# Weight sums in 28 steps on VectorE over two chunks, the split two periods ahead of its inverse, and gelu written into the products' tile

## The chip, the cores and the metric

The kernel runs on one core of a Trainium2 chip. The metric is the device time of one execution in microseconds, lower is better. A core has five engines, each with its own queue of instructions, kept in order: TensorE (PE, matmuls; its weight loads run beside it), VectorE (DVE), ScalarE (ACT), GpSimd (POOL) and SyncE (SP), which here only issues DMAs. Engines wait for each other by semaphores. PE writes into PSUM, whose eight banks are reused; everything else lies in SBUF.

## The reference

One block over 8192 tokens of width 448: adaptive layer norm, a spectral mixer (2D FFT, a two-layer block MLP in the frequency domain, inverse FFT), a residual, a second layer norm, and a gated feed-forward net of width 1792.

```python
sa, ca, ga, sb, cb, gb = (silu(c) @ w_mod) in six parts
h = layernorm(x) * (1 + ca) + sa
x = x + ga * irfft2(block_mlp(rfft2(h)))
h = layernorm(x) * (1 + cb) + sb
x = x + gb * ((gelu(h @ w_gate) * (h @ w_up)) @ w_down)
```

## The kernel before

The first part (forward transform, MLP in frequency, first half of the inverse) ends at about 385 us of the profile, and the change doesn't touch it. The second part runs over 32 chunks of 256 tokens (`CB` = 2 rows of 128 by `nch` = 32). For each chunk it does the second half of the inverse transform, the residual and the layer norm; it casts the result to a high and a low f16 part (`pack_hi`, `pack_lo`, tile `pk`), transposes it by DMA into `nt` (tiles of 128 columns at the places `UN`, `NU` of them), multiplies by the gate and up weights (high part `wh`, low part `wl`), and by the down weights. Products are made of f16 pairs: high by high, high by low, low by high.

The 1792 columns are seven pairs `t` of two blocks of 128. Two ways are used for gate and up:

- The first four chunks (`C0` = 4) are plain: `gate_up(i, k)` over 14 steps k, then `gate_up_out`: gelu on ScalarE (L1215, into a tile `gel`), the product gate by up on VectorE (L1224, into a tile `x` of eight blocks), and four sums of blocks on GpSimd (`out_sums`, L1232 to L1235). `quantize` makes the f16 pair of a finished `x`: the high part on ScalarE (L1240), the low part on VectorE (L1244).
- From the fifth chunk on, each 2 by 2 block product takes seven products in place of eight (Strassen's scheme). It needs sums of the input blocks (`combos`) and of the weight blocks (tiles `sh`). `period(n, hook)` is the unit of this part: pair n enters with `front1` and `front2`, pair n-1 passes `mid`, pair n-2 finishes with `back_e` and `back_d` (gelu, product, sums of each half), and pairs n-3 and n-4 are quantized. The PSUM banks go round in a ring with three E and three D slots: `front1` can take its E slot only when the product on VectorE of the period before has read it.

`down(i-1)` (seven products of the down weights, output stored at L1466) is written after step k = 2 of a plain chunk and after the period t = 2 of a later one.

The weight sums for the seven products are made once. `make_s` (four 128x128 adds on GpSimd, L1398 to L1401, then a high part on ScalarE, L1391, and a low part of 384 columns on VectorE, L1392) runs at the steps of chunk 2, and `make_s1` (one add, L1404, its result written over weights in `wh` and `wl` that plain chunks no longer need) at those of chunk 3 and in the first period. 42 loads of raw weights (L1388) go through SyncE into a tile `rc` of two buffers.

What else a chunk needs is placed by hand. `hooks` holds, by step k, what is done in plain chunks for later chunks; `hooks2` does so for the periods, where k = 2t + j, with j = 0 after `mid` and j = 1 at the end of the period. An entry's first number says how many chunks ahead it works. `split_g` and `split_v` cast the inverse's operand and take its low part on ScalarE (L123) and GpSimd (L125: `gl`, `vn`); `inverse` is L1036 to L1038. `transposes_dma` (L1146) puts the transposes of the next chunk into SyncE's queue; in later chunks 16 of 22 go at k = 4, and six behind the output store. SyncE works its queue in order, so each transfer waits for those issued ahead of it, and each of those for its buffer.

Of the kernel before, what the change touches and what calls it, by code (L numbers as in the profile page):

```python
# [39 lines left out]
NU = 24  # L40
UN = [0, 2, 16, 18, 20, 8, 10, 22]
# [18 lines left out]
def spectral_geglu(ctx, tc, x, wt_in, wgu, wd, cvec, wmod, cf1, cs2, cmi, cgm, out):  # L60
# [924 lines left out]
    with ExitStack() as cctx:  # L985
# [4 lines left out]
        cp.tile([128, H], F32, tag="gel", name="gel", bufs=2)  # L990
# [17 lines left out]
        def x8():  # L1008
            return cp.tile([128, 8, 128], F32, tag="x8", name="x8", bufs=3)
# [106 lines left out]
        def pack_lo(i):  # L1116
# [10 lines left out]
            if i > 0:  # L1127
                nt_tile(i)
# [7 lines left out]
        def transposes_dma(i, lo=0, hi=None):  # L1136
            todo = [(UN[t] + b, source(i, t, b)) for t in range(8) for b in range(2) if i < C0 or (t, b) not in ((0, 1), (5, 1))]
            if i >= C0:
                pk = nxt[i]["pk"]
                todo += [  # L1140
                    (8 * l + 4 + j, pk[:, l * NF + 2 * D + j * 128 : l * NF + 2 * D + (j + 1) * 128])
                    for l in range(2)
                    for j in range(4)
                ]
# [66 lines left out]
        gels = {}  # L1211

        def out_gelu(i, t, q, ps):
            gl = cp.tile([128, H], F32, tag="gel", name="gel", bufs=2)
            S.activation(gl, ps[:, :H], AF.Gelu_apprx_tanh, scale=dg)  # L1215
            gels[(i, t, q)] = gl

        def out_mult(i, t, q, ps):
            gl = gels.pop((i, t, q))
            if (i, t) not in acts:  # L1220
                acts[(i, t)] = x8()
            x = acts[(i, t)]
            dst = x[:, 1:3] if q else x[:, 0::7]
            V.tensor_tensor(  # L1224
                dst, ps[:, H : 2 * H].rearrange("p (b c) -> p b c", b=2), gl.rearrange("p (b c) -> p b c", b=2), ALU.mult
            )
# [47 lines left out]
        def prod(c, ps, b, w, u, start=False):  # L1274

            nt = nts[c[0]]
            for pr in range(2):
                o = ps[:, pr * H + b * 128 : pr * H + (b + 1) * 128]
                for n, (l, v) in enumerate(((0, u), (0, u + 8), (1, u))):
# [38 lines left out]
        def front1(a):  # L1318
# [4 lines left out]
            prod(a, e, 0, a_of(t, 1, 0), 4)  # L1323
# [5 lines left out]
        def front2(a):  # L1329
            prod(a, es[a], 1, s_of(a[1], 0), 5)  # L1330
            V.tensor_tensor(quarter(ds[a], 1), quarter(es[a], 1), c5s[a], ALU.add)  # L1331

        def mid(b):
            e = es[b]
            prod(b, e, 1, s_of(b[1], 2), 6)
# [3 lines left out]
        def back_e(c):  # L1339
            e = es[c]  # L1340
            prod(c, e, 0, a_of(c[1], 1, 1), 7)
# [16 lines left out]
        def period(n, hook):  # L1358
# [25 lines left out]
        def load_s(t, pr, lo):  # L1384
            raws_s[(t, pr)] = r = sp.tile([128, 512], F32, tag="rc", name="rc", bufs=2).rearrange("p (i k c) -> p i k c", i=2, k=2)
            for i in range(lo, 2):
                m = t + NP * i
                dma(r[:, i], wgu[m // 2, pr, :, 0:2, (m % 2) * 128 : (m % 2) * 128 + 128])  # L1388

        def w_split(hi, lo, src, pr):  # L1390
            S.activation(hi, src, AF.Copy, scale=sw[:, pr : pr + 1])  # L1391
            V.scalar_tensor_tensor(lo, src, sw[:, pr : pr + 1], hi, op0=ALU.mult, op1=ALU.subtract)  # L1392

        def make_s(t, pr):
            r = raws_s.pop((t, pr)).rearrange("p i k c -> p (i k) c")
            if pr == 0:
                shs[t] = sp.tile([128, 2, 2, 3, 128], F16, name=f"sh{t}")
            G.tensor_tensor(r[:, 3], r[:, 2], r[:, 3], ALU.add)  # L1398
            G.tensor_tensor(r[:, 2], r[:, 0], r[:, 2], ALU.subtract)
            G.tensor_tensor(r[:, 0], r[:, 3], r[:, 0], ALU.subtract)  # L1400
            G.tensor_tensor(r[:, 1], r[:, 1], r[:, 0], ALU.subtract)  # L1401
# [305 lines left out]
```

## Time and profile before

| | us |
|---|---|
| median of 3 runs | 2112.77 |
| lowest and highest run | 2112.22, 2117.72 |
| the profiled execution's own time | 2107.65 |
| span of the profile, first to last instruction | 2105.9 |
| mean granted TensorE clock, share of full | 0.957 |

In the profile's page an engine's row tells its busy time, its share of the span, and its instructions. A string of 40 digits cuts the span into equal slices, each digit the busy share in tenths. Rows of waits say which line of an engine waited, for which line of which engine, how long in total, how often, and the longest. Rows of a timeline give start, length, engine, line, operation, output from input, and in brackets the idle time ahead and what ended it.

### The profile page before, as it was taken

The numbers are of one execution on the slowest core, as the hardware profiler recorded it, in microseconds if no ns is written. First come the engines' busy times: TensorE is split into PE (matmuls) and PEld (weight loads), VectorE is DVE, ScalarE is ACT, GpSimd is POOL, SyncE is SP. The second block draws the span as 40 slices with busy tenths as digits, with TensorE's granted clock in tenths as the row PEclk, the third lists the DMA queues.
The fourth block names the chain that finished last, engine by engine and source line by source line (L and its number), as shares of the span: only waits on it lengthen the run. The fifth ranks groups of instructions, "written<-read, shape, count | busy, mean of one in ns | idle before, by whom it ended". The sixth has DMA issues, their size and how long they took to land.

```text
span 2105.9 us, 51710 instructions
## 1 busy us (share of the span) xinstructions
PE 1940.9 (92%) x21137; PEld 1706.1 (81%) x21137; DVE 1298.7 (62%) x2877; ACT 981.3 (47%) x1942; POOL 1252.8 (59%) x1591
## 2 busy tenths in 40 slices
PE   7899999896676999999999999999999999999998
PEld 3689999685465888888888888888888888888897
DVE  8687898772525555666655655665566556655544
ACT  6677887431323444444444444444444444444433
POOL 4466796353754566666665666666666666666544
PEclk9899999898888999999999999999999999999999
DMA  9988786411121111111111111111111111111100
GB/s 389 289 273 236 206 229 173 127 41 53 57 63 48 45 44 44 44 54 45 45 45 45 53 50 49 44 44 44 44 44 44 44 45 44 45 44 45 26 19 19
DMA packets 182739, 175.95 MB, mean 84 GB/s; under 512 B 112614, under 2 KB 155366, under 8 KB 182118
## 3 DMA queue, kind: packets, MB, share of 16 engines
q1 hardware_dynamic: 182502, 172.65, 27.8%
q8 instruction: 165, 2.70, 0.5%
q14 instruction: 72, 0.59, 0.1%
HBM read 103.79 MB, written 47.25 MB: 72 GB/s over the span
## 4 chain that ended last, share of the span: by engine, by line
PE 36%; POOL 28%; ACT 7%; DVE 5%; issue 3%; SPq 2%; DMA 1%; POOLq 0%; ACTq 0%
POOL x L1232 9%; PE pdn L1414 7%; PE pdn L1416 7%; PE pdn L1415 7%; PE ring L1280 6%; PE ring L1294 6%; ACT ac L1240 4%; POOL x L1233 4%; POOL pk L1126 3%; POOL x L1235 3%; DVE x L1224 3%; POOL vn L125 3%; ACT gel L1215 2%; SPq L1146 2%; POOL x L1234 2%
## 5 line engine op out<-in xcount | busy, mean ns | idle before, releaser
L1232 POOL TENSOR_TENSOR x<-x 128x128 f32<-128x128 f32 x223 | 275.9, 1237 | 328.5 <-DVE x L1224 320.2
L1414 PE MATMUL pdn<-wd,ac 128*128 128x224 f16 x1568 | 409.2, 261 | 23.9 <-ACT p L1445 18.1
L1416 PE MATMUL pdn<-wd,ac 128*128 128x224 f16 x1568 | 408.9, 261 | 6.5 <-DVE ac L1244 6.5
L1415 PE MATMUL pdn<-wd,ac 128*128 128x224 f16 x1568 | 409.1, 261 | 0.0
L1294 PE MATMUL ring<-nt,wh 128*128 128x256 f16 x2352 | 379.4, 280 | 0.0
L1224 DVE TENSOR_TENSOR x<-ring,gel 128x256 f32<-128x256 f32 x392 | 164.6, 420 | 308.7 <-ACT gel L1215 308.7
L1280 PE MATMUL ring<-nt,wh 128*128 128x128 f16 x3136 | 332.8, 222 | 11.2 <-DVE x L1224 11.2
L1244 DVE SCALAR_TENSOR_TENSOR ac<-x,sa_act,ac 128x896 f16<-128x896 f32 (+1 forms) x226 | 315.8, 1399 | 13.8 <-ACT ac L1240 13.8
L1280 PE MATMUL ring<-nt,sh 128*128 128x128 f16 x3528 | 298.6, 221 | 13.8 <-ACT rc L1327 13.6
L1240 ACT ACTIVATE ac<-x,sa_act 128x896 f16<-128x896 f32 (+1 forms) x226 | 233.9, 1036 | 141.4 <-POOL x L1235 141.2
L1280 PE MATMUL ring<-nt,wl 128*128 128x128 f16 x1568 | 298.7, 222 | 0.0
L1215 ACT ACTIVATE gel<-ring,dg 128x256 f32<-128x256 f32 x392 | 183.7, 469 | 197.9 <-PE ring L1309 163.3
L1280 PEld LDWEIGHTS <-wh 128*128 128x128 f16 x3136 | 251.9, 99 | 27.2 <-issue 23.7
L1280 PEld LDWEIGHTS <-sh 128*128 128x128 f16 x3528 | 217.3, 99 | 63.7 <-issue 63.7
L1294 PEld LDWEIGHTS <-wh 128*128 128x128 f16 x2352 | 220.3, 101 | 22.0
L1325 ACT COPY ring<-ring 128x256 f32<-128x256 f32 x196 | 70.0, 357 | 325.1 <-PE ring L1280 249.8
L1294 PE MATMUL ring<-nt,wl 128*128 128x256 f16 x784 | 219.3, 280 | 0.0
L1458 POOL TENSOR_TENSOR vo<-u,p 128x224 f32<-128x224 f32 x32 | 21.4, 668 | 298.0 <-DVE u L1457 298.0
L1415 PEld LDWEIGHTS <-ac 128*128 128x128 f16 x1568 | 154.5, 99 | 20.0 <-issue 18.3
L1331 DVE TENSOR_TENSOR ring<-ring,rc 128x256 f32<-128x256 f32 x196 | 84.4, 430 | 125.2 <-PE ring L1280 125.0
L1416 PEld LDWEIGHTS <-ac 128*128 128x128 f16 x1568 | 154.6, 99 | 8.6 <-DVE ac L1244 7.9
L1414 PEld LDWEIGHTS <-ac 128*128 128x128 f16 x1568 | 154.5, 99 | 7.6 <-ACT ac L1240 6.3
(313 smaller groups left out, 4385.4 us busy)
## 6 DMA issues: line engine op xcount, KB each, us to landing
raw<-in_gu SPq DMA_DIRECT2D x28, 512.0 KB, 5.3
vd<-us SPq DMA_DIRECT2D x64, 224.0 KB, 3.4
v<-vd SPq DMA_DIRECT2D x64, 224.0 KB, 2.8
x<-in_x SPq DMA_DIRECT2D x31, 448.0 KB, 4.5
out<-x SPq DMA_DIRECT2D x31, 448.0 KB, 2.6
nt<-pk SPq DMA_TRANSPOSE x656, 2.3
tr<-td SPq DMA_DIRECT2D x22, 448.0 KB, 7.0
tb<-in_x SPq DMA_DIRECT2D x8, 896.0 KB, 17.7
```

Source lines behind the costliest of these rows:

```text
L1215: S.activation(gl, ps[:, :H], AF.Gelu_apprx_tanh, scale=dg)
L1224: V.tensor_tensor(dst, ps[:, H : 2 * H].rearrange("p (b c) -> p b c", b=2), gl.rearrange("p (b c) -> p b c", b=2), ALU.mult)
L1232: e.tensor_tensor(s1, a21, a22, ALU.add)
L1233: e.tensor_tensor(s2, s1, a11, ALU.subtract)
L1240: S.activation(acq[(i, t)][:, 0, k], acts[(i, t)][:, k], AF.Copy, scale=sa_act[:, t : t + 1])
L1244: V.scalar_tensor_tensor(ac[:, 1, k], acts[(i, t)][:, k], sa_act[:, t : t + 1], ac[:, 0, k], op0=ALU.mult, op1=ALU.subtract)
L1280: T.matmul(o, w(l, pr), nt[:, v * 128 : (v + 1) * 128], start=start and pr == 0 and n == 0, stop=n == 2, skip_group_check=True,)
L1294: T.matmul(ps[:, pr * H : (pr + 1) * H], w[:, tw, f0 : f0 + 128], nt[:, UN[tn] * 128 : UN[tn] * 128 + H], start=False, stop=True, skip_gro ...
L1331: V.tensor_tensor(quarter(ds[a], 1), quarter(es[a], 1), c5s[a], ALU.add)
L1414: T.matmul(ps, ac[:, 0, ka], wds[t][:, 0, kb], start=t == 0, stop=False)
L1415: T.matmul(ps, ac[:, 0, ka], wds[t][:, 1, kb], start=False, stop=False)
L1416: T.matmul(ps, ac[:, 1, ka], wds[t][:, 0, kb], start=False, stop=t == NP - 1)
```

## The change

- **Weight sums.** All four sums of a pair get a place in `sh` (512 columns, the fourth is now `s_of(t, 3)`), so nothing in `wh` or `wl` is written over and `make_s1` is gone. The four adds run on VectorE. `sums_step` counts steps: an even one makes the high part of one sum and issues two loads for the next (28 in all), an odd one makes the low part. It is called at three places of `down(1)` and `down(2)`, at the steps 1 to 13 of chunk 2 and at the steps of chunk 3, 33 places for the 30 steps that are needed.
- **Gelu.** It is written straight into the products' tile `x`, and the product is taken in place. The tile `gel` is gone, and `x` has two buffers for three.
- **Plain chunks' transposes.** The next chunk's are issued four at a time at k = 0, 3, 5 and 7, the rest at k = 9, where all were issued at k = 0.
- **Later chunks.** The split is at k = 0 (period t = 0) for k = 2 (t = 1); the inverse stays at k = 4 (t = 2). `pack_hi` and `pack_lo` are at k = 10 and 11 (t = 5) for 12 and 13 (t = 6). `load_v` and `load_g` are written in another place, but stand at the same place in SyncE's queue.
- **`nt` is narrower** (22 places for 24), so `UN` and the indices of the products' operands are renumbered; `nt_tile` is taken in `transposes_dma`.
- **The end.** A high and a low quantization that were done twice are done once, and the high one stands behind the last gelu in the last two periods.

```diff
...
@@ -989,3 +989,2 @@
         wds = wds + [cp.tile([128, 2, 7, HC], F16, name=f"wd{t}") for t in range(len(wds), NP)]
-        cp.tile([128, H], F32, tag="gel", name="gel", bufs=2)
         x1t, nts, acts, acq, pgu = {}, {}, {}, {}, {}
@@ -1008,3 +1007,3 @@
         def x8():
-            return cp.tile([128, 8, 128], F32, tag="x8", name="x8", bufs=3)
+            return cp.tile([128, 8, 128], F32, tag="x8", name="x8", bufs=2)
 
@@ -1126,4 +1125,2 @@
                 e.tensor_tensor(pk[:, NF + c.start : NF + c.stop], n[:, c], pk[:, c], ALU.subtract)
-            if i > 0:
-                nt_tile(i)
 
@@ -1136,2 +1133,4 @@
         def transposes_dma(i, lo=0, hi=None):
+            if i not in nts:
+                nt_tile(i)
             todo = [(UN[t] + b, source(i, t, b)) for t in range(8) for b in range(2) if i < C0 or (t, b) not in ((0, 1), (5, 1))]
...
@@ -1210,18 +1209,14 @@
 
-        gels = {}
+        def out_of(i, t, q):
+            x = acts[(i, t)]
+            return x[:, 1:3] if q else x[:, 0::7]
 
         def out_gelu(i, t, q, ps):
-            gl = cp.tile([128, H], F32, tag="gel", name="gel", bufs=2)
-            S.activation(gl, ps[:, :H], AF.Gelu_apprx_tanh, scale=dg)
-            gels[(i, t, q)] = gl
-
-        def out_mult(i, t, q, ps):
-            gl = gels.pop((i, t, q))
             if (i, t) not in acts:
                 acts[(i, t)] = x8()
-            x = acts[(i, t)]
-            dst = x[:, 1:3] if q else x[:, 0::7]
-            V.tensor_tensor(
-                dst, ps[:, H : 2 * H].rearrange("p (b c) -> p b c", b=2), gl.rearrange("p (b c) -> p b c", b=2), ALU.mult
-            )
+            S.activation(out_of(i, t, q), ps[:, :H].rearrange("p (b c) -> p b c", b=2), AF.Gelu_apprx_tanh, scale=dg)
+
+        def out_mult(i, t, q, ps):
+            x = out_of(i, t, q)
+            V.tensor_tensor(x, ps[:, H : 2 * H].rearrange("p (b c) -> p b c", b=2), x, ALU.mult)
 
...
@@ -1322,3 +1317,3 @@
             prod(a, e, 1, a_of(t, 0, 0), 0, True)
-            prod(a, e, 0, a_of(t, 1, 0), 4)
+            prod(a, e, 0, s_of(t, 3), 1)
             d = ds[a] = ring("D", n)
...
@@ -1374,3 +1369,3 @@
                 out_mult(*c, 1, es.pop(c))
-            if pair(n - 3):
+            if pair(n - 3) and a:
                 quant_hi(*pair(n - 3))
@@ -1379,2 +1374,4 @@
                 del ds[c]
+            if pair(n - 3) and not a:
+                quant_hi(*pair(n - 3))
             hook(1)
@@ -1383,27 +1380,35 @@
 
-        def load_s(t, pr, lo):
-            raws_s[(t, pr)] = r = sp.tile([128, 512], F32, tag="rc", name="rc", bufs=2).rearrange("p (i k c) -> p i k c", i=2, k=2)
-            for i in range(lo, 2):
+        def load_s(t, pr):
+            raws_s[(t, pr)] = r = sp.tile([128, 512], F32, tag="rc", name="rc", bufs=2).rearrange("p (i c) -> p i c", i=4)
+            for i in range(2):
                 m = t + NP * i
-                dma(r[:, i], wgu[m // 2, pr, :, 0:2, (m % 2) * 128 : (m % 2) * 128 + 128])
-
-        def w_split(hi, lo, src, pr):
-            S.activation(hi, src, AF.Copy, scale=sw[:, pr : pr + 1])
-            V.scalar_tensor_tensor(lo, src, sw[:, pr : pr + 1], hi, op0=ALU.mult, op1=ALU.subtract)
+                dma(r[:, 2 * i : 2 * i + 2], wgu[m // 2, pr, :, 0:2, (m % 2) * 128 : (m % 2) * 128 + 128])
 
         def make_s(t, pr):
-            r = raws_s.pop((t, pr)).rearrange("p i k c -> p (i k) c")
+            r = raws_s[(t, pr)]
             if pr == 0:
-                shs[t] = sp.tile([128, 2, 2, 3, 128], F16, name=f"sh{t}")
-            G.tensor_tensor(r[:, 3], r[:, 2], r[:, 3], ALU.add)
-            G.tensor_tensor(r[:, 2], r[:, 0], r[:, 2], ALU.subtract)
-            G.tensor_tensor(r[:, 0], r[:, 3], r[:, 0], ALU.subtract)
-            G.tensor_tensor(r[:, 1], r[:, 1], r[:, 0], ALU.subtract)
-            w_split(shs[t][:, 0, pr], shs[t][:, 1, pr], r[:, 0:3], pr)
-
-        def make_s1(t, pr):
-            r = raws_s.pop((t, pr))
-            G.tensor_tensor(r[:, 1, 0], r[:, 1, 0], r[:, 1, 1], ALU.add)
-            w = a_of(t, 1, 0)
-            w_split(w(0, pr), w(1, pr), r[:, 1, 0], pr)
+                shs[t] = sp.tile([128, 2, 2, 4, 128], F16, name=f"sh{t}")
+            V.tensor_tensor(r[:, 3], r[:, 2], r[:, 3], ALU.add)
+            V.tensor_tensor(r[:, 2], r[:, 0], r[:, 2], ALU.subtract)
+            V.tensor_tensor(r[:, 0], r[:, 3], r[:, 0], ALU.subtract)
+            V.tensor_tensor(r[:, 1], r[:, 1], r[:, 0], ALU.subtract)
+            S.activation(shs[t][:, 0, pr], r, AF.Copy, scale=sw[:, pr : pr + 1])
+
+        def make_s_lo(t, pr):
+            r, sh = raws_s.pop((t, pr)), shs[t]
+            V.scalar_tensor_tensor(sh[:, 1, pr], r, sw[:, pr : pr + 1], sh[:, 0, pr], op0=ALU.mult, op1=ALU.subtract)
+
+        steps = itertools.count()
+
+        def sums_step():
+            m, r = divmod(next(steps), 2)
+            item = divmod(m - 1, 2)
+            if r:
+                if 0 < m <= NFT:
+                    make_s_lo(*item)
+                return
+            if 0 < m <= NFT:
+                make_s(*item)
+            if m < NFT:
+                load_s(*divmod(m, 2))
 
@@ -1434,2 +1439,4 @@
             def extra(key):
+                if C0 - 3 <= i < C0 - 1 and key in ("b2", "u2", "u4"):
+                    sums_step()
                 for fn, *args in second.get(key, []) if i == 0 else amid.get(key, []) if new and i + 3 < nch else []:
@@ -1475,9 +1482,9 @@
         hooks = {
-            0: [(1, transposes_dma)],
-            3: [(2, only, True, split_g), (2, only, True, split_v)],
-            5: [(2, only, False, split_g), (2, only, False, split_v)],
+            0: [(1, transposes_dma, 0, 4)],
+            3: [(1, transposes_dma, 4, 8), (2, only, True, split_g), (2, only, True, split_v)],
+            5: [(1, transposes_dma, 8, 12), (2, only, False, split_g), (2, only, False, split_v)],
             6: [(2, only, True, inverse)],
-            7: [(2, only, False, inverse), (2, residual)],
+            7: [(1, transposes_dma, 12, 16), (2, only, False, inverse), (2, residual)],
             8: [(2, stats2)],
-            9: [(2, rsqrt_part, 5)],
+            9: [(1, transposes_dma, 16), (2, rsqrt_part, 5)],
             10: [(2, rsqrt_part, 9)],
@@ -1489,6 +1496,6 @@
         hooks2 = {
-            2: [(2, split_g), (2, split_v)],
+            0: [(2, split_g), (2, split_v)],
             4: [(1, transposes_dma, 0, 16), (2, inverse, slice(0, D), "pd"), (2, residual)],
-            12: [(2, pack_hi)],
-            13: [(2, pack_lo)],
+            10: [(2, pack_hi)],
+            11: [(2, pack_lo)],
         }
@@ -1556,5 +1563,8 @@
         def run_hooks(table, i, k):
-            if k == (2, 1, 0)[min(i, 2)] and i + 2 < nch:
+            if i < C0 and k == (2, 1, 0)[min(i, 2)]:
                 load_v(i + 2)
                 load_g(i + 2)
+            if i >= C0 - 1 and k == 10 and i + 3 < nch:
+                load_v(i + 3)
+                load_g(i + 3)
             for d, fn, *args in table.get(k, []):
@@ -1576,14 +1586,4 @@
                 run_hooks(hooks, i, k)
-                t, pr = divmod(k, 2)
-                if i == C0 - 2:
-                    if k > 0:
-                        make_s(*divmod(k - 1, 2))
-                    load_s(t, pr, 0)
-                if i == C0 - 1:
-                    if k == 0:
-                        make_s(NP - 1, 1)
-                    elif k > 1:
-                        make_s1(*divmod(k - 2, 2))
-                    if k > 0:
-                        load_s(*divmod(k - 1, 2), 1)
+                if i == C0 - 1 or (i == C0 - 2 and k > 0):
+                    sums_step()
         for n in range(C0 * NP, nch * NP + 2):
@@ -1592,8 +1592,2 @@
             def hook(j):
-                if n == C0 * NP:
-                    if j == 0:
-                        make_s1(NP - 1, 0)
-                        load_s(NP - 1, 1, 1)
-                    else:
-                        make_s1(NP - 1, 1)
                 if i < nch:
@@ -1606,4 +1600,3 @@
                     transposes_dma(i + 1, 16)
-        quant_lo(nch - 1, NP - 3)
-        quantize(nch - 1, NP - 2)
+        quant_lo(nch - 1, NP - 2)
         quantize(nch - 1, NP - 1, (0, 3, 7))
```

Three places in the order of instructions. First ScalarE in a later chunk, around the cast of the next tile to be transposed (`ring` is a PSUM slot, `gel` the gelu's tile, `x_...` a products' tile, `ac` the quantized one). Before:

```order
L1215 ACTIVATE gel<-ring,dg 128x256 [waits PE_49]
L1240 ACTIVATE ac<-x_18220,sa_act 128x896 [waits Pool_49]
L1215 ACTIVATE gel<-ring,dg 128x256 [waits PE_49]
L1325 COPY ring<-ring 128x2x128 [waits DVE_49,PE_49]
L1327 COPY rc<-ring 128x256
L1336 COPY ring<-ring 128x2x128 [waits PE_49]
L1113 CAST pk<-vn 128x1280 [waits DMAHW4_49,DMAHW5_49,DMAHW3_49,DMAHW6_49,DMAHW2_49,DMAHW7_49,DMAHW1_49,DMAHW0_49]
L1215 ACTIVATE gel<-ring,dg 128x256 [waits PE_49]
L1240 ACTIVATE ac<-x_18302,sa_act 128x896 [waits Pool_49]
L1215 ACTIVATE gel<-ring,dg 128x256 [waits PE_49]
L1325 COPY ring<-ring 128x2x128 [waits DVE_49,PE_49]
L1327 COPY rc<-ring 128x256
```

And now:

```order
L1217 ACTIVATE x_17926<-ring,dg 128x256 [waits DVE_49,PE_49]
L1235 ACTIVATE ac<-x_17846,sa_act 128x896 [waits Pool_49]
L1217 ACTIVATE x_17926<-ring,dg 128x2x128 [waits PE_49]
L1320 COPY ring<-ring 128x2x128 [waits DVE_49,PE_49]
L1322 COPY rc<-ring 128x256
L1331 COPY ring<-ring 128x2x128 [waits PE_49]
L1112 CAST pk<-vn 128x1280 [waits DMAHW4_49,DMAHW5_49,DMAHW3_49,DMAHW6_49,DMAHW2_49,DMAHW7_49,DMAHW1_49,DMAHW0_49]
L1217 ACTIVATE x_18015<-ring,dg 128x256 [waits DVE_49,PE_49]
L1235 ACTIVATE ac<-x_17926,sa_act 128x896 [waits Pool_49]
L1217 ACTIVATE x_18015<-ring,dg 128x2x128 [waits PE_49]
L1320 COPY ring<-ring 128x2x128 [waits DVE_49,PE_49]
L1322 COPY rc<-ring 128x256
```

The cast of `pk` waits for eight DMA queues, those of the transposes that read the tile. The rows around it read alike, but its place has moved: counted from the down stage's last copy (L1450), three periods of six rows and three copies of the next stood ahead of it, and now two periods and three copies. Behind it stand the same two gelus and the quantization; the first gelu now waits for VectorE too. The casts `gh` and `vo` of the split stand a period earlier too, in period t = 0.

Second SyncE, from the plain chunk 2 to the first of the later chunks (`nt<-pk` are transposes, `rc<-in_gu` loads of raw weights, `out` the store of a chunk). Before:

```order
L1146 DMA_TRANSPOSE nt<-pk 128x128 x16
L1388 DMA rc<-in_gu 128x2x128 x4
L1466 DMA out<-x_5668 128x896
L1388 DMA rc<-in_gu 128x2x128 x24
L929 DMA v<-vd 128x2x224 x2
L918 DMA g<-cgm 128x256
L923 DMA x_7797<-in_x 128x896
L1146 DMA_TRANSPOSE nt<-pk 128x128 x22
L1388 DMA rc<-in_gu 128x2x128
L1466 DMA out<-x_5860 128x896
L1388 DMA rc<-in_gu 128x2x128 x13
L929 DMA v<-vd 128x2x224 x2
```

And now:

```order
L1145 DMA_TRANSPOSE nt<-pk 128x128 x4
L1385 DMA rc<-in_gu 128x2x128 x4
L1473 DMA out<-x_5667 128x896
L1385 DMA rc<-in_gu 128x2x128 x2
L1145 DMA_TRANSPOSE nt<-pk 128x128 x4
L1385 DMA rc<-in_gu 128x2x128 x2
L1145 DMA_TRANSPOSE nt<-pk 128x128 x4
L1385 DMA rc<-in_gu 128x2x128 x2
L1145 DMA_TRANSPOSE nt<-pk 128x128 x4
L1385 DMA rc<-in_gu 128x2x128 x6
L929 DMA v<-vd 128x2x224 x2
L918 DMA g<-cgm 128x256
```

The 16 transposes that stood in one row ahead of the first weight loads now stand in fours between them, and the loads between two stores are fewer.

Third VectorE, in `down(1)` and the steps behind it (`rc` the raw weights, `sh` the sums, `vo` and `u` the down stage's parts). Now:

```order
L1453 TENSOR_TENSOR vo<-pdn,p_7033 128x224
L1458 TENSOR_TENSOR u_7035<-pdn,p_7033 128x224
L1391 TENSOR_TENSOR rc<-rc 128x128
L1392 TENSOR_TENSOR rc<-rc 128x128
L1393 TENSOR_TENSOR rc<-rc 128x128
L1394 TENSOR_TENSOR rc<-rc 128x128
L1460 TENSOR_TENSOR u_7036<-pdn,u_7035 128x224
L1399 SCALAR_TENSOR_TENSOR sh_7130<-rc,sw,sh_7130 128x512
L1463 TENSOR_TENSOR vo<-pdn,u_7036 128x224
L1464 TENSOR_TENSOR u_7035<-pdn,u_7035 128x224
L1470 TENSOR_TENSOR vo<-pdn,u_7036 128x224
L1391 TENSOR_TENSOR rc<-rc 128x128
```

The four adds, which GpSimd had, stand between the down stage's own adds, the products of the plain steps and their quantization.

More of the change, by code (lines that the diff above doesn't have):

```diff
@@ L39 @@
 NF = 2 * D + 512
-NU = 24
-UN = [0, 2, 16, 18, 20, 8, 10, 22]
+NU = 22
+UN = [0, 2, 14, 16, 18, 7, 9, 20]
 LAM = 0.01
@@ L1140, in transposes_dma @@
                 todo += [
-                    (8 * l + 4 + j, pk[:, l * NF + 2 * D + j * 128 : l * NF + 2 * D + (j + 1) * 128])
+                    (7 * l + (1, 4, 5, 6)[j], pk[:, l * NF + 2 * D + j * 128 : l * NF + 2 * D + (j + 1) * 128])
                     for l in range(2)
@@ L1278, in prod @@
                 o = ps[:, pr * H + b * 128 : pr * H + (b + 1) * 128]
-                for n, (l, v) in enumerate(((0, u), (0, u + 8), (1, u))):
+                for n, (l, v) in enumerate(((0, u), (0, u + 7), (1, u))):
                     T.matmul(
@@ L1329, in front2 @@
         def front2(a):
-            prod(a, es[a], 1, s_of(a[1], 0), 5)
+            prod(a, es[a], 1, s_of(a[1], 0), 4)
             V.tensor_tensor(quarter(ds[a], 1), quarter(es[a], 1), c5s[a], ALU.add)
@@ L1334, in mid @@
             e = es[b]
-            prod(b, e, 1, s_of(b[1], 2), 6)
+            prod(b, e, 1, s_of(b[1], 2), 5)
             S.copy(quarter(e, 0), quarter(e, 1))
@@ L1340, in back_e @@
             e = es[c]
-            prod(c, e, 0, a_of(c[1], 1, 1), 7)
+            prod(c, e, 0, a_of(c[1], 1, 1), 6)
             rest(c, 1, e)
```

## The prediction

> **What bounds the kernel now.** I read the page first: its span, the engines' shares and the two strings of 40 slices.
>
> ```profile
> span 2105.9 us, 51710 instructions
> PE 1940.9 (92%) x21137; PEld 1706.1 (81%) x21137; DVE 1298.7 (62%) x2877; ACT 981.3 (47%) x1942; POOL 1252.8 (59%) x1591
> PE   7899999896676999999999999999999999999998
> ```
>
> A slice is 52.6 us. TensorE (PE) is at 9 almost everywhere but dips to 6 to 8 in slices 9 to 13, from about 421 to 684 us: there the four plain feed-forward chunks end and the seven-product chunks begin. The changed lines lie from there to the end. What comes before 440 us I count as unchanged.
>
> Next, windows over that stretch (columns: window, its length, then busy us of PE, weight loads, VectorE, ScalarE, GpSimd, the granted clock, DMA share, GB/s), and what PE waited for from 430 to 700 us.
>
> ```profile
> 480.00:540.00 60.00, 34.36 (x307) 29.94 (x304) 13.90 (x23) 10.96 (x19) 26.39 (x43) 0.84 0.18 50
> 540.00:600.00 60.00, 42.93 (x305) 33.73 (x305) 25.43 (x54) 16.26 (x28) 39.51 (x67) 0.79 0.22 61
> 600.00:660.00 60.00, 38.89 (x328) 31.72 (x326) 26.48 (x64) 18.68 (x37) 35.15 (x50) 0.83 0.14 41
> 660.00:700.00 40.00, 36.38 (x412) 32.80 (x411) 20.07 (x55) 12.34 (x30) 17.54 (x22) 0.91 0.23 61
> PE pdn L1414 <- ACT p L1445: 18.1, 1, 18.1
> PE pgu L1171 <- DVE x L1224: 13.2, 7, 3.6
> PE ring L1280 <- ACT rc L1327: 13.0, 2, 10.2
> PE pi L1036 <- ACT vo L123: 6.5, 2, 5.3
> ...
> PE ring L1261 <- DVE x L1224: 4.5, 1, 4.5
> ```
>
> In 220 us PE is busy 152.6, so it idles 67.4; and the missing clock costs its busy time another 34.4 x 0.16 + 42.9 x 0.21 + 38.9 x 0.17 + 36.4 x 0.09 = 24 us. No single engine is full there: the queues hold each other up. The 18.1 us show how. SyncE (SP) issues transposes and weight loads in one queue:
>
> ```profile
> 459.85 0.52 SPq L1466 DMA_DIRECT2D out<-x  x1
> 481.88 20.87 SPq L1146 DMA_TRANSPOSE nt<-pk  x16
> 502.79 2.12 SPq L1388 DMA_DIRECT2D rc<-in_gu  x4
> 523.80 0.36 SPq L1466 DMA_DIRECT2D out<-x  x1
> 524.33 53.98 SPq L1388 DMA_DIRECT2D rc<-in_gu  x24
> ...
> 610.08 0.41 SPq L1466 DMA_DIRECT2D out<-x  x1
> 691.26 0.35 SPq L1466 DMA_DIRECT2D out<-x  x1
> 508.03 0.61 ACT L1391 ACTIVATE sh<-rc,sw 128x384 f16<-128x384 f32 x1 [23.01 <-POOL rc L1401]
> 509.30 0.35 PE L1414 MATMUL pdn<-wd,ac 128*128 128x224 f16 x1 [18.10 <-ACT p L1445]
> ```
>
> The first weight load stands behind 20.87 us of transposes; ScalarE waits 23.01 us for the sums that GpSimd makes of it, and the copy that frees PE's bank stands behind on ScalarE. The output stores mark the chunks: 63.95, 86.28 and 81.18 us between these four.
>
> Then the steady chunks: the waits of PE from 700 us on, a window of one chunk, one without a clock dip, and the dip itself.
>
> ```profile
> PE pi L1038 <- POOL vn L125: 39.3, 25, 1.6
> ...
> 1282.80:1334.10 51.30, 49.31 (x590) 43.61 (x588) 30.70 (x68) 22.45 (x47) 31.50 (x41) 0.97 0.17 45
> 872.00:923.30 51.30, 49.31 (x602) 44.05 (x603) 32.32 (x72) 22.46 (x48) 33.03 (x44) 1.00 0.17 46
> 1329.25:1332.75 3.50, 3.50 (x25) 2.30 (x25) 1.39 (x3) 0.37 (x1) 3.42 (x6) 0.51 0.14 28
> 1328.35 0.47 PE L1038 MATMUL pi<-vn,gh 128*128 128x448 f32 x1 [1.56 <-POOL vn L125]
> ```
>
> PE idles 1.99 of 51.3 us: 1.56 for the low part of the inverse's operand, the other 0.4 for the E slot of the ring, which the product on VectorE frees. After the 1.56 us wait the clock stands at 0.51 for 3.5 us, some 1.7 us of work lost. So a chunk without idle time and dip is 51.3 - 1.99 - 1.7 = 47.6 us; three of the steady intervals have no dip, near 49.7.
>
> **The change, part by part.**
>
> *The sums and their loads (three intervals).* GpSimd loses the 28 groups of four adds and the 14 single ones; VectorE gains 28 x 4 adds (112). Their like on VectorE is the 128x128 add of the combinations:
>
> ```profile
> 1293.70 0.28 DVE L1100 TENSOR_TENSOR vn<-vn 128x128 f32<-128x128 f32 x1
> 474.52 0.93 PE L1171 MATMUL pgu<-nt,wh 128*128 128x256 f16 x7
> ...
> 475.61 0.93 PE L1171 MATMUL pgu<-nt,wh 128*128 128x256 f16 x7
> 508.68 0.62 DVE L1392 SCALAR_TENSOR_TENSOR sh<-rc,sw,sh 128x384 f16<-128x384 f32 x1 [21.08 <-ACT sh L1391]
> ```
>
> That is 4 x 0.28 + about 0.8 for the low part (0.62 scaled by 512/384) = 1.9 us on VectorE per weight sum, 54 us in all, in windows where VectorE is busy 14 to 26 of 60 us: it fits. Loads fall from 42 to 28. The transposes are cut into fours, so an SP turn of two steps is four transposes at 1.3 (20.87/16) and two loads at 0.5 (2.12/4): 6.2 us. Two plain steps hold 44 matmuls (1232 in the 56 steps of four chunks), and ten of them take 475.61 - 474.52 = 1.09: 4.8 us. SP is therefore a little late, and a make_s that waits for its load holds VectorE's queue, with the products and the down stage's adds behind it; I give this 5 us over the two chunks. The split of the plain chunks isn't moved, so of its wait (the 6.5 row) 5 us stay. The first two periods fill the ring: the 10.2 us wait was for sums that come last in the queue; with the sums ended by step 10 of chunk 3 I leave 5 us of it and of the 4.5. 15 of the 67 us of waits stay, so I leave a third of the clock's 24, 8. That is 23 of 91 us: **gain 68 us**, the three intervals together 163 for 231.4. Bounds: at best all 91 but the ring's start, 86; at worst, if every make_s waits behind SP as the first one does now and only the 18.1 us go, 20. I stay by the row of 18.1 and the SP rows, which say the delay came of order, not of bytes.
>
> *Gelu in the products' tile, two tiles for three.* The gelu of the second half must wait for the low quantization two pairs earlier. That stands at the head of VectorE's period:
>
> ```profile
> 1307.42 1.14 DVE L1244 SCALAR_TENSOR_TENSOR ac<-x,sa_act,ac 128x896 f16<-128x896 f32 x1
> 1308.12 0.39 ACT L1336 COPY ring<-ring 128x256 f32<-128x256 f32 x1
> 1309.00 0.47 ACT L1215 ACTIVATE gel<-ring,dg 128x256 f32<-128x256 f32 x1 [0.49 <-PE ring L1309]
> 1312.75 0.39 ACT L1336 COPY ring<-ring 128x256 f32<-128x256 f32 x1
> 1313.05 1.26 ACT L1113 CAST pk<-vn 128x1280 f16<-128x1280 f32 x1
> 1302.05 7.51 SPq L1146 DMA_TRANSPOSE nt<-pk  x6
> 1321.31 2.58 DVE L1244 SCALAR_TENSOR_TENSOR ac<-x,sa_act,ac 128x896 f16<-128x896 f32 x1
> 1326.21 2.08 POOL L125 TENSOR_TENSOR vn<-v,vo 128x896 fp32r<-128x896 f32 x1
> ```
>
> It ends at 1308.56, before the gelu starts at 1309.00: free, with 0.44 us to spare. Where GpSimd's long pack subtraction runs, it takes 2.58 us and the gelu waits about half a microsecond, once a chunk.
>
> *The split two steps earlier (25 chunks).* Two steps are one period, 1312.75 - 1308.12 = 4.63 us. GpSimd's low part of the operand, 1.56 us late now, so comes 3.1 us ahead of the inverse: the 39.3 us go. GpSimd's queue keeps its length; its pack subtraction moves by a period too.
>
> *The pack two steps earlier.* This is what I set against it. The cast (L1113) writes the tile that the last six transposes of the chunk before read. They are issued until 1309.56, and land, with the 2.3 us of the page's row for transposes counted from the last one's issue at 1308.3, at about 1310.65. Now the cast is issued at 1313.05, free. Two steps earlier it stands behind the copy at 1308.12, ready at 1308.4, and waits 2.25 us for the landing; then 1.26 us of its own. Queued behind it on ScalarE is the gelu of 1309.00, which comes at 1311.9, so 2.9 us late; behind that the product on VectorE, and behind that the E slot that the next front1 on PE needs. Of the 2.9 us the ring's slack takes 0.8; **PE waits 2.1 us** in the following period. The GpSimd and VectorE loop (product, low part, sums, high part, gelu, which follow each other without a gap) gives the 4.63 us of the period, and PE's own matmuls fill all but 0.1 of it. It has no room to catch up, so I add 0.4, 0.7 and 0.1 us in the next three periods: 3.3 us. A chunk is then 47.0 (the 47.6 less the pipe's refill of 0.6 after the two waits that are gone) + 3.3 = 50.3, and with a dip after the 2.1 us wait, mostly beside ScalarE's lateness, 50.8. By the window 51.24 now (the median between stores). The gain is 0.45 x 22 - 1.1 x 3 (those without a dip now) = about **7 us**, with bounds from -35 (a full dip and none of the lateness hidden: +1.4 a chunk) to +100 (the cast's wait doesn't reach PE: 47.0).
>
> *The end.* The doubled quantizations go and the last gelu no longer stands behind a high part:
>
> ```profile
> 2085.97 0.37 PE L1416 MATMUL pdn<-wd,ac 128*128 128x224 f16 x1 [4.69 <-DVE ac L1244]
> ```
>
> Of the 4.69 us about 3 go (a low part of 1.14, a high part of the like and the gelu's place): bounds 0 and 4.7.
>
> *Sum.* 68 + 7 + 3 = 78 us from the profiled execution, which took 2107.65 us (span 2105.9): 2029.6. It lies 5.1 us below the median of the three runs; I keep half of that, as the change shortens the stretch with most waits: a median of about 2032.
>
> [...]
>
> **The rivals.**
>
> 1. *The cast doesn't reach PE* (0.2). The ring is three slots deep, and ScalarE is busy 22 of 51 us, which speaks for it; the E wait in every chunk, 0.42 us, speaks against. A chunk is 47.0 to 48.5: 2.7 to 4.2 x 25 = 68 to 105 us instead of 7: 1935 to 1971.
> 2. *Slower: the two tiles bind in every period.* If in the new order the low quantization takes 2.58 us in each period, not once a chunk, the gelu waits 2.58 - 1.14 - 0.44 = 1.0 us in each of some 175 periods, and with the loop as long as the period nothing takes it up: +175 us, less 71 of the rest: about 2214. It beats the gain from 71/175 = 0.41 us a period on. Against it: the 2.58 comes only beside GpSimd's 128x1280 subtraction. 0.04.
> 3. *The sums stay late* (0.12): VectorE's queue waits for SP as GpSimd's did, and of the 68 us only 20 to 40 come: 2060 to 2080.
> 4. *The cast costs more than the wait it replaces* (0.17): a dip in every chunk, and nothing of the lateness hidden, +0.4 to +1.4 a chunk: 2049 to 2074.
> 5. *No dip at all* (0.12): with the 1.56 us wait gone and 2.1 us split over several, the clock stays up, as in the window from 872: 50.3 in all chunks, 12 us less: 2020. [...]
>
> That the change doesn't do what it says I give nothing of its own: the order of the instructions shows the cast and the splits moved.
>
> **How the numbers follow.** My forecast, with terms of 68, 7 and 3, has 0.35 and by itself covers 2012 to 2050. It is the likeliest, so the time is 2032. The range of 8 in 10: rival 1 reaches lowest, and half of it (0.1) lies above 1950; rivals 3 and 4 end by 2080; so 1950 to 2080. A measurement of this kernel can tell about 0.3% (6 us) from no change. Slower than 2119 would need rival 2, or rivals 3 and 4 together at their worst (20 - 35 + 0 = -15): 0.04. Within 0.3% only by the last two in milder form: 0.03. Faster: 0.93.
>
> **What would show it.** The rows of waits: the 18.1 us wait gone and the stores of the three transition intervals near 44, 55 and 63 us; if they stand near 64, 75 and 75, rival 3 holds. In a steady chunk no wait of L1038 for `vn`, and instead a wait of PE's ring for `x` of about 2 us in the period after the cast, with the cast itself waiting for the transposes about 2.2 us; a chunk of 50.3 to 50.8 between stores. If that wait is missing and the chunk is under 48.5, rival 1 holds; if all gelus wait for the low part, rival 2; if the clock is 1.00 in chunk windows, rival 5. I would be wrong most of all in how far the cast's 2.9 us run through ScalarE's queue, as no row of the trace shows such a wait.

## The result, and the profile after

The changed kernel takes 2077.38 us (median of 4 runs, 2075.73 to 2082.39), the kernel before 2112.49 (4 runs). The ratio is 0.9833, 95% interval 0.9809 to 0.9857: 35 us less, where 81 were forecast. The time lies within the stated range of 1950 to 2080, near its upper end.

The page after, against the same rows of before:

```profile
span 2073.4 us, 51742 instructions
PE 1929.5 (93%) x21137; PEld 1716.6 (83%) x21137; DVE 1291.9 (62%) x2918; ACT 979.6 (47%) x1927; POOL 1225.3 (59%) x1521
PE   7899999898879999999999999999999999999998
```

The dip of slices 9 to 13 is shorter and shallower, not gone. SyncE's timeline of the same stretch shows the chunks by their stores (L1473):

```profile
459.77 0.52 SPq L1473 DMA_DIRECT2D out<-x  x1
...
482.28 5.75 SPq L1145 DMA_TRANSPOSE nt<-pk  x4
488.08 2.12 SPq L1385 DMA_DIRECT2D rc<-in_gu  x4
503.97 0.36 SPq L1473 DMA_DIRECT2D out<-x  x1
...
570.35 0.36 SPq L1473 DMA_DIRECT2D out<-x  x1
...
641.78 0.35 SPq L1473 DMA_DIRECT2D out<-x  x1
...
2031.73 0.34 SPq L1473 DMA_DIRECT2D out<-x  x1
```

The first weight load is issued at 488.08, behind 5.75 us of transposes instead of 20.87. The three intervals are 44.2, 66.4 and 71.4 us, together 182.0 for 231.4: **49.4 us gained** (68 forecast). From the fourth store to the last one shown it is 1389.95 us. Before it was 1368.16 us, from 691.26 to this row of the kernel before:

```profile
2059.42 0.34 SPq L1466 DMA_DIRECT2D out<-x  x1
```

That is **21.8 us lost** in 27 intervals (7 gained forecast). Behind the last store 41.7 us remain for 46.5: **4.8 gained** (3 forecast). The sum is 32.4, and the spans differ by 32.5.

PE's waits after, from 430 to 700 us (line, what it waited for, us in total, times, longest):

```profile
PE pgu L1170 <- DVE x L1221: 6.3, 3, 4.3
PE ring L1275 <- DVE x L1221: 4.9, 2, 3.8
PE ring L1275 <- ACT rc L1322: 3.9, 1, 3.9
PE ring L1275 <- DVE ring L1326: 3.4, 1, 3.4
...
PE ring L1256 <- DVE x L1221: 2.5, 1, 2.5
```

From 700 us on only one kind is left above 1.3 us:

```profile
PE ring L1275 <- DVE x L1221: 70.9, 25, 3.7
```

The 18.1 us wait and, in the steady chunks, the 39.3 us for `vn` are gone. In their place stands one wait a chunk for a product on VectorE, 70.9/25 = 2.84 us. One steady chunk's timelines show where it comes from: the transposes on SyncE, ScalarE around the cast, VectorE and PE behind it:

```profile
1262.74 7.51 SPq L1145 DMA_TRANSPOSE nt<-pk  x6
1268.82 0.39 ACT L1331 COPY ring<-ring 128x256 f32<-128x256 f32 x1
1273.01 1.26 ACT L1112 CAST pk<-vn 128x1280 f16<-128x1280 f32 x1 [3.80 <-DMA v<-vd]
1274.18 0.47 ACT L1217 ACTIVATE x<-ring,dg 128x256 f32<-128x256 f32 x1
1274.68 0.42 DVE L1221 TENSOR_TENSOR x<-ring,x 128x256 f32<-128x256 f32 x1 [4.11 <-ACT x L1217]
1275.16 0.37 PE L1275 MATMUL ring<-nt,wh 128*128 128x128 f16 x2 [3.51 <-DVE x L1221]
```

Read it downwards: the copy ends at 1269.2, the cast starts at 1273.0, the gelu behind it at 1274.2, its product at 1274.7, and PE, which needs the E slot, at 1275.2. The window of this chunk (columns as before) and the cast's waits on ScalarE from 700 to 1900 us:

```profile
1262.34:1314.59 52.25, 48.74 (x590) 44.06 (x588) 29.50 (x68) 22.62 (x47) 31.45 (x41) 0.97 0.17 44
```

```profile
ACT pk L1112 <- DMA nt<-pk: 51.4, 17, 4.0
ACT pk L1112 <- issue: 19.9, 6, 3.9
ACT pk L1112 <- DMA v<-vd: 3.8, 1, 3.8
```

The cast waits 75.1 us in 24 chunks, 3.1 each. One is put down to the load of `v` and six to no releaser; that it is the transposes in all of them is for an experiment to show.

### The profile page after: what moved, and what is told of

Read it like the earlier page. It is cut to its first block, busy times and chain, and to the rows that moved or that the text cites. A ratio compares the mean times of both kernels' runs of the same rounds, so it can differ in the third digit from the quotient of the medians.

```text
span 2073.4 us, 51742 instructions
## 1 busy us (share of the span) xinstructions
PE 1929.5 (93%) x21137; PEld 1716.6 (83%) x21137; DVE 1291.9 (62%) x2918; ACT 979.6 (47%) x1927; POOL 1225.3 (59%) x1521
## 4 chain that ended last, share of the span: by engine, by line
PE 50%; SPq 9%; POOL 8%; DVE 6%; issue 4%; DMA 3%; ACT 2%; ACTq 0%; POOLq 0%
PE ring L1275 15%; PE ring L1289 10%; SPq L1145 8%; PE pdn L1421 6%; PE pdn L1419 6%; PE pdn L1420 6%; POOL x L1435 3%; POOL vo L1434 3%; PE pgu L1170 2%; DMA nt<-pk 2%; PE ring L1304 2%; ACT x L1217 1%; DVE ac L1239 1%; DVE x L1221 1%; POOL vo L1465 1%
## 5 line engine op out<-in xcount | busy, mean ns | idle before, releaser
L1221 DVE TENSOR_TENSOR x<-ring,x 128x256 f32<-128x256 f32 x392 | 165.2, 422 | 359.2 <-ACT x L1217 356.6
L1275 PE MATMUL ring<-nt,sh 128*128 128x128 f16 x4704 | 377.5, 225 | 7.3 <-ACT rc L1322 3.9
L1275 PE MATMUL ring<-nt,wh 128*128 128x128 f16 x2352 | 272.8, 226 | 75.9 <-DVE x L1221 75.9
L1275 PEld LDWEIGHTS <-sh 128*128 128x128 f16 x4704 | 294.4, 101 | 54.2 <-issue 54.2
L1239 DVE SCALAR_TENSOR_TENSOR ac<-x,sa_act,ac 128x896 f16<-128x896 f32 (+1 forms) x225 | 285.8, 1271 | 16.6 <-ACT ac L1235 16.6
L1275 PEld LDWEIGHTS <-wh 128*128 128x128 f16 x2352 | 195.4, 101 | 90.0 <-issue 86.2
L1217 ACT ACTIVATE x<-ring,dg 128x256 f32<-128x256 f32 x392 | 183.9, 469 | 181.7 <-PE ring L1304 119.7
L1289 PEld LDWEIGHTS <-wh 128*128 128x128 f16 x2352 | 220.0, 101 | 21.6
L1275 PE MATMUL ring<-nt,wl 128*128 128x128 f16 x1176 | 237.7, 226 | 0.0
```

The lines of the kernel that those rows point to most:

```text
L1217: S.activation(out_of(i, t, q), ps[:, :H].rearrange("p (b c) -> p b c", b=2), AF.Gelu_apprx_tanh, scale=dg)
L1221: V.tensor_tensor(x, ps[:, H : 2 * H].rearrange("p (b c) -> p b c", b=2), x, ALU.mult)
L1239: V.scalar_tensor_tensor(ac[:, 1, k], acts[(i, t)][:, k], sa_act[:, t : t + 1], ac[:, 0, k], op0=ALU.mult, op1=ALU.subtract)
L1275: T.matmul(o, w(l, pr), nt[:, v * 128 : (v + 1) * 128], start=start and pr == 0 and n == 0, stop=n == 2, skip_group_check=True,)
L1289: T.matmul(ps[:, pr * H : (pr + 1) * H], w[:, tw, f0 : f0 + 128], nt[:, UN[tn] * 128 : UN[tn] * 128 + H], start=False, stop=True, skip_gro ...
```

## Experiments

Each was timed against the kernel before on the same chip; its median there was 2109.0, 2109.1 and 2108.7 us in the three sessions. Ratios are to it.

### The pack put back, in the changed kernel

```diff
 hooks2
-            10: [(2, pack_hi)],
-            11: [(2, pack_lo)],
+            12: [(2, pack_hi)],
+            13: [(2, pack_lo)],
```

> The changed kernel with the pack put back to k = 12 and 13; the split stays at k = 0. Theory 1 (the cast of pk waits on ScalarE for the last six transposes, holds a gelu back, PE waits 2.8 us a chunk and loses another 1.7 us to the clock's dip): the cast waits for nothing, no wait of PE over 0.5 us in a chunk, 47.1 to 48.5 us between stores in place of 51.5, about 1975 to 2005 us. Theory 2 (the two products' tiles, or the VectorE and GpSimd loop, pace the chunk, and the cast's wait only takes the place of another): stays over 50 us a chunk, 2050 us or more.

2022.06 us, ratio 0.9589 (0.9570 to 0.9608), by the ratios some 51 us less than the change as it is. The stores stand 49.7 us apart in nearly all steady chunks, between the two expectations: the cast's wait is gone, but a new one stands there. PE's waits from 700 to 1900 us, a window over some four chunks, and the timeline where the new one comes about:

```profile
PE ring L1275 <- ACT rc L1322: 42.8, 24, 1.8
```

```profile
1000.00:1200.00 200.00, 191.13 (x2363) 171.62 (x2361) 121.54 (x274) 90.18 (x190) 126.39 (x165) 1.00 0.17 46
```

```profile
1215.70 1.04 ACT L1235 ACTIVATE ac<-x,sa_act 128x896 f16<-128x896 f32 x1 [3.89 <-POOL x L1230]
1218.35 0.49 PE L1275 MATMUL ring<-nt,sh 128*128 128x128 f16 x6 [1.77 <-ACT rc L1322]
```

With the pack in the period t = 6 and the split in t = 0, GpSimd has its long subtraction and the split's low parts in neighbouring periods; its sums come late, the high part on ScalarE waits 3.89 us for them, the copies stand behind it, and PE waits 1.8 us for a copy. I had not foreseen this wait, in the prediction or here. The clock is 1.00. The same wait stands in the next run, where the split is moved and the pack is at k = 12, and it shrinks to 0.7 us (20.3/30) with the pack at k = 11, further below.

### The split alone, in the kernel before

```diff
 hooks2
-            2: [(2, split_g), (2, split_v)],
+            0: [(2, split_g), (2, split_v)],
```

> The kernel before with the split alone put to k = 0; the pack stays at k = 12, three products' tiles and the gelu's own tile stay. Theory 1: the wait for vn goes and the dip with it, 47.1 to 48.5 us between stores for 51.24, 2015 to 2045 us; the interval of a chunk equals that of the changed kernel with its pack put back, within 0.3 us, if the two tiles cost nothing. Theory 2: over 50 us a chunk, 2085 us or more.

2082.37 us, ratio 0.9868 (0.9851 to 0.9886), between the two expectations. The stores stand 49.7 us apart, as in the run above, and PE's largest wait from 700 to 1900 us is the same:

```profile
PE ring L1280 <- ACT rc L1327: 42.7, 24, 1.8
```

So the split earlier takes 1.5 us off a chunk, not 3 to 4, and the two tiles with the gelu in place cost nothing here: this kernel has three tiles and the run above two, with 49.7 in both. In both it is the wait for ScalarE's copy that stands in the chunk, so a smaller cost of the tiles could hide behind it. The third interval rose to 86.4 us from 81.2; I have no run that says why.

### The pack alone, in the kernel before

The edit is that of the change (`pack_hi`, `pack_lo` at 10 and 11), the split stays at 2.

> The kernel before with the pack alone put to k = 10 and 11; the split stays at k = 2. Theory 1: the wait for vn (1.56 us) stays, and the cast's stall of about 2.8 us comes on top, 54 us between stores, or 55.6 with a second dip; 2180 to 2220 us. Theory 2: within 10 us of before, 2100 to 2125 us.

2155.47 us, ratio 1.0215 (1.0187 to 1.0244): slower, as expected of the cast's stall, but by 46 us and not by 70 to 110. PE's waits from 700 to 1900 us:

```profile
PE ring L1280 <- DVE x L1224: 68.4, 35, 3.8
PE pi L1038 <- POOL vn L125: 17.0, 23, 0.8
```

The stall came, and because PE is late from it, the wait for `vn` shrank from 1.56 to 17.0/23 = 0.74 us. The chunks are mostly 52.2 to 52.8 us.

This run also shows two things about the dip. Two successive chunks, with the wait for `x` in each (windows, then PE's timeline):

```profile
749.16:801.47 52.31, 47.86 (x590) 42.70 (x588) 30.67 (x68) 22.41 (x47) 31.47 (x41) 1.00 0.17 44
801.47:853.75 52.28, 49.07 (x590) 43.51 (x588) 29.55 (x68) 22.42 (x47) 31.48 (x41) 0.97 0.16 44
761.04 0.27 PE L1280 MATMUL ring<-nt,wh 128*128 128x128 f16 x2 [2.57 <-DVE x L1224]
813.33 0.27 PE L1280 MATMUL ring<-nt,wh 128*128 128x128 f16 x2 [2.56 <-DVE x L1224]
```

A wait of 2.57 us draws no dip and one of 2.56 us draws one. And the two chunks are equally long: with the dip PE is busy 1.2 us more and waits that much less. Here the dip costs nothing.

### The transposes ahead of the store, in the changed kernel

```diff
 down(i), in place of the call behind it
+            if new and not last:
+                transposes_dma(i + 2, 16) if i + 2 < nch else None
             if not last:
                 dma(ov[:, i * CB : (i + 1) * CB, :], x1)
```

> The changed kernel with the last six transposes of a chunk issued ahead of the output store in SyncE's queue, nothing else. Theory 1: they start some 2.2 us earlier, so the cast's wait falls from 3.1 to about 1 us, PE's wait under 0.7 us, the chunk to 47.5 to 49.5 us, the time to 1980 to 2030. If the cast waits for something else (the loads of v behind the transposes, as one row has it, or an older transpose): its wait stays near 3 us and the time within 10 us of 2077.

1995.21 us, ratio 0.9454 (0.9434 to 0.9473). All 22 transposes of the chunk shown run without a gap, and the store, which waits for GpSimd (58.2 us in 23 waits on SyncE from 700 to 1900 us of the changed kernel), no longer holds six of them back. The timelines of SyncE and ScalarE, and PE's waits from 700 to 1900 us:

```profile
1204.69 29.95 SPq L1145 DMA_TRANSPOSE nt<-pk  x22
1234.74 0.52 SPq L1475 DMA_DIRECT2D out<-x  x1
1236.00 1.26 ACT L1112 CAST pk<-vn 128x1280 f16<-128x1280 f32 x1 [0.15 <-issue]
```

```profile
PE ring L1275 <- ACT rc L1322: 14.4, 25, 0.6
PE ring L1275 <- DVE x L1221: 10.8, 29, 1.3
```

The cast's wait falls to 0.15 us here, PE's waits from 2.84 to about 1.0 us a chunk. Since only the transposes and the store changed places, it was the transposes that the cast waited for. By the ratios some 80 us come back.

### The pack half a period later, in the changed kernel

```diff
 hooks2
-            10: [(2, pack_hi)],
-            11: [(2, pack_lo)],
+            11: [(2, pack_hi)],
+            12: [(2, pack_lo)],
```

> The changed kernel with the pack half a period later, at k = 11 and 12; the store stays ahead of the six transposes, the split stays at k = 0. If the cast's lateness alone is what PE pays for: at k = 11 it is issued some 2.3 us later, behind the gelus of its period, so its wait of 3.1 us shrinks under 1 us and PE's wait of 2.8 us a chunk under 1; 47.5 to 49.5 us between stores, 1985 to 2025 us. If what PE pays for is that cast, casts of the split and the long subtraction stand in neighbouring periods, as with the pack at k = 12 (49.73 us a chunk): 49.5 us or more, 2015 us or more.

1990.35 us, ratio 0.9436 (0.9417 to 0.9454), 48.4 us a chunk: some 84 us by two numbers in a table. The cast stands behind the gelus, and mostly finds its transposes landed: from 700 to 1900 us it waits 7.0 us in 8 chunks, for 75.1 in 24. PE's largest wait from 700 to 1900 us:

```profile
PE ring L1275 <- ACT rc L1322: 20.3, 30, 2.6
```

One chunk between its stores:

```profile
738.69:787.06 48.37, 47.48 (x590) 42.86 (x588) 30.53 (x68) 22.58 (x47) 31.44 (x41) 1.00 0.18 48
```

### The transposes of the plain chunks spread, in the kernel before

```diff
 hooks
-            0: [(1, transposes_dma)],
+            0: [(1, transposes_dma, 0, 4)],
...
+            3, 5, 7: four more each; 9: the rest
```

> The kernel before with the plain chunks' transposes alone issued at k = 0, 3, 5, 7 and 9 for all at k = 0. If the 18.1 us wait came of the first weight load standing behind 16 transposes: the first of the three intervals between stores falls from 64 to 45 to 50 us, the other two move by under 5 us, the time to 2085 to 2100. If the sums on GpSimd are what held it: first interval over 58 us, time within 8 us of before.

2100.08 us, ratio 0.9948 (0.9925 to 0.9971). The time is at the upper end of the first expectation. The first interval falls from 64.0 to 47.0 us, as expected of the load behind the transposes. The second is 85.4 (86.3); the third rises from 81.2 to 89.3, against the expectation. Alone, spreading gives back there half of what it brings.

### The adds back on GpSimd, in the changed kernel

The four `V.tensor_tensor` of `make_s` become `G.tensor_tensor`.

> The changed kernel with the four adds of a weight sum back on GpSimd; the single pass of 28 steps, the places of the steps and the spread transposes stay. If the engine is what was gained: the three intervals go from 44, 66 and 71 us towards 45, 80 and 78, and the time rises by 15 to 25 us. If the gain came of the single pass (28 loads and steps for 42) and the spread transposes: the intervals within 4 us each, the time within 8 us of 2077.

2084.06 us, ratio 0.9871 (0.9852 to 0.9891), whose interval just meets that of the change (0.9809 to 0.9857). The three intervals are 43.8, 74.6 and 75.0 us: 11.4 more than with VectorE, between the two expectations. So of the 49.4 us gained there the engine is some 11, and 38 come of the rest of the change. Spreading alone, in the run above, took 10 off the three intervals; most of the 38 is therefore the single pass, or the pass and the spreading together; that the gelu in place or the moved split have no part in it was not tested.

### The high part of a sum one step later, in the changed kernel

```diff
 ...
 sums_step
             if r:
                 if 0 < m <= NFT:
-                    make_s_lo(*item)
+                    make_s_hi(*item)
                 return
             if 0 < m <= NFT:
                 make_s(*item)
+            if 1 < m <= NFT + 1:
+                make_s_lo(*divmod(m - 2, 2))
```

> The changed kernel with the high part of a weight sum on ScalarE taken one step later (and its low part with the next sum's adds), so that no gelu stands behind it in the step of its adds. If the second interval (66 us, where 45 would do) is paced by one serial loop, adds on VectorE, high part and gelu on ScalarE, product and low part on VectorE, adds: it falls to 52 to 58, the third from 71 to 62 to 68, the time to 2055 to 2067. If SyncE's queue, the inverse's operand or the clock paces it: each interval within 3 us, the time within 6 us of 2077.

2065.98 us, ratio 0.9787 (0.9767 to 0.9808), some 10 us less than the change. The second interval falls from 66.4 to 59.6, the third from 71.4 to 68.7. Both end a little above the ranges that a pure serial loop gave (52 to 58, 62 to 68), so the loop is there and is not all. It is seen in the changed kernel's timelines of VectorE, ScalarE and PE:

```profile
535.70 0.72 ACT L1395 ACTIVATE sh<-rc,sw 128x512 f16<-128x512 f32 x1 [4.44 <-DVE rc L1394]
536.32 0.46 ACT L1217 ACTIVATE x<-pgu,dg 128x256 f32<-128x256 f32 x1
536.81 0.42 DVE L1221 TENSOR_TENSOR x<-pgu,x 128x256 f32<-128x256 f32 x1 [1.15 <-ACT x L1217]
537.29 0.48 PE L1170 MATMUL pgu<-nt,wl 64*128 64x256 f16 x5 [1.27 <-DVE x L1221]
```

ScalarE sits idle 4.44 us in front of the sum's high part, which waits for the adds; the gelu runs right behind it, the product waits for the gelu, and PE for the product. VectorE's share of busy time (44.5 of 66.4 us) doesn't show this.

### Both, and the later pack too

> Both: the six transposes ahead of the store (measured alone: 1995 us) and the high part a step later. The two act on different chunks, so their gains add: 1975 to 1987 us if the later high part brings what the serial loop says, 1992 to 1998 if it brings nothing.

1987.27 us, ratio 0.9404 (0.9376 to 0.9431), just above the first expectation. Against the swap alone (0.9454) that is again some 10 us: the gains add.

> The six transposes ahead of the store, the high part of the sums a step later, and the pack at k = 11 and 12: the cast of pk never waits. Against the same with the pack at k = 10 (1987 us): 5 to 15 us less if the cast's remaining waits (0.4 us in 16 of 25 chunks) start what is left in a chunk; 5 to 15 us more if the later subtraction on GpSimd meets the split of the next period and holds the sums.

1978.72 us, ratio 0.9392 (0.9363 to 0.9422). It is the fastest kernel of the study, by the ratios some 93 us faster than the change, but the intervals of these two overlap, so whether the pack's place still matters beside the swap stays open.

## Why the prediction was wrong

Two terms failed. The step that gave the wrong sign is the cost of the earlier pack in a steady chunk: I let PE wait 2.1 us for the held-up gelu and gave 0.5 us to the clock's dip behind it; PE waited 2.84 us and the dip took about 1.3, so a chunk took 51.5 us instead of 50.8, and 21.8 us were lost where 7 were to be gained. The transition's term of 68 us had the right mechanism and was too large by 19. That the time still lies in the range is due to the width of the range, not to the working.

**The transition, 68 us: right in its mechanism, mis-sized at 49.4.** The load behind the transposes was the cause of the 18.1 us wait, and spreading alone showed it (64.0 to 47.0). What I left of the loss, 23 of 91, was too little. I had left 5 us for the ring's start; its four waits are 3.9, 3.4, 2.5 and 1.1 (the shorter of the two in the 4.9), together 10.9. I had left 5 us for the inverse's operand; its waits in the three intervals are 8.2. I had left 5 us for make_s behind its loads; what came was another thing, the gelu behind the sum's high part on ScalarE, and it showed as 6.3 us at `pgu`: with the high part a step later these fell to 2.3, and of the 6.8 us that the second interval lost, 4.1 were idle time of PE and 2.7 busy time, at a clock of 0.94 for 0.87. The waits after sum to some 27 us in the three intervals where I left 15, and the clock's loss, 55.1 x 0.13 + 57.0 x 0.14 = 15, is twice my 8. The windows of the second and third interval, and then, of the kernel with the high part a step later, the second:

```profile
503.97:570.35 66.38, 55.05 (x464) 45.77 (x462) 44.52 (x98) 22.68 (x37) 35.73 (x42) 0.87 0.24 67
570.35:641.78 71.43, 56.99 (x528) 48.93 (x527) 47.91 (x107) 22.43 (x42) 37.13 (x45) 0.86 0.19 49
```

```profile
500.61:560.20 59.59, 52.33 (x464) 44.56 (x462) 43.54 (x98) 22.23 (x35) 33.25 (x42) 0.94 0.27 75
```

The count of the sums was wrong as well: there are 14, not 28, so 56 adds on VectorE, not 112, and some 27 us by the forecast's own 1.9 us each, not 54. No term of the sum hangs on it, only the judgement that the work fits.

**The steady chunks, +7 us: the sign was wrong.** The steps one by one:

- *The split earlier ends the wait for `vn`*: right, no such row is left after 700 us.
- *The cast waits for the last six transposes and PE pays*: right, and shown by the swap. The sizes were not: the cast waits 3.1 us, not 2.25, PE 2.84, not 2.1. I took the transposes' 7.51 us from one chunk. In the chunks of before they take 7.49 to 9.47 us, with a median of 8.2; my row was nearly the shortest. The landing varies too: in the chunk shown above the six took 7.51 us again, but the cast started 2.76 us behind their end, where 1.2 to 1.5 us is usual. From the first of the six to the cast it is mostly about 9.5 us after the change, where I had 8.6. The longest, in SyncE's timeline of the kernel before:

```profile
1814.49 9.47 SPq L1146 DMA_TRANSPOSE nt<-pk  x6
```

- *0.4, 0.7 and 0.1 us in the next three periods*: not there. PE has no other wait of note in the chunk.
- *A dip after the wait, mostly hidden beside ScalarE's lateness*: mis-sized. PE is busy 48.74 us in the chunk shown, at a clock of 0.97, and 47.48 us in a chunk of the kernel with the later pack, at 1.00: the dip adds about 1.3 us of busy time where I had left 0.5. Every one of the 25 chunks has a dip (mean clock 0.94 to 0.97), so no chunk of this kernel shows what it would take without one; when the swap ends the wait, dip and wait go together (clock 1.00 from 800 to 1300 us).
- The sum: 48.74 + 2.84 = 51.6 us, and 51.5 is the median of the 25 intervals. Four of them, at a clock of 0.94, take 52.9 to 53.7. Against my 50.8 the base of 47.0 is 0.5 short: no run shows the 0.6 us that I took off for the pipe's refill; at full clock PE is busy 47.69 us in a chunk of the kernel before, with both its waits, and 47.48 us in one with the later pack. The wait is 0.7 short and the dip 0.8, and the next three periods' 1.2 didn't come. The last interval but one pays for wait and dip as well, 50.0 us for 47.0 before; I had no term for it.
- *Two tiles cost nothing*: right as far as shown (49.7 with two and with three).

Rival 4, to which I gave 0.17, is what happened here; the time is still 3 us above its bounds, as the transition fell short too. Rival 1's bound (47.0) stayed out of reach even without the cast's stall, 48.4 at best, since about 1 us of waits for ScalarE and VectorE is left.

**The end, 3 us**: 4.8, at its upper bound of 4.7.

## What to carry to other kernels

An operation that is moved earlier in a queue kept in order takes its waits with it, as the cast did with 3.1 us a chunk: ask when each of its inputs and its buffer come free at the new place, and what stands behind it. Here half a period, or the order of two transfers on another queue, was worth some 84 and 80 us. Take the length of a step from all its repetitions when the slack is of the size of their spread, and don't take the clock loss behind a stall for hidden, or for paid, before a run shows it: with the pack alone it was hidden, and before the change it was paid (51.24 us with it, 49.68 without).

## What the runs showed of the hardware

**The clock's dip doesn't follow the length of a wait alone.** With the pack alone, a wait of 2.57 us drew none and one of 2.56 us did (rows in that section). In the kernel before, a wait of 1.56 us drew the dip in 21 chunks, and four chunks with the same wait had none (49.68 us, clock 1.00). With the pack put back, a wait of 1.77 us drew none in the window of some four chunks shown there, at a clock of 1.00. What decides was not shown.

**Some of VectorE's adds are slow beside GpSimd.** Of the changed kernel's 56 adds of 128x128, 37 took 0.26 to 0.31 us. Of those beside operations of GpSimd with two inputs, five took 1.10 to 1.17 us and two 2.04 and 2.05, one of them in these rows of its timelines of VectorE and GpSimd:

```profile
515.98 2.05 DVE L1394 TENSOR_TENSOR rc<-rc 128x128 f32<-128x128 f32 x1
515.76 2.12 POOL L125 TENSOR_TENSOR vn<-v,vo 128x896 fp32r<-128x896 f32 x1
```

I had costed all adds at 0.28; their mean is 0.47.
